# Fifteen small loads of B_x in front of the last three pieces of w4 on the SP queue

## The chip, the cores and the metric

The kernel runs on one core of a Trainium2 chip. The metric is the device time of one execution in microseconds (us). Several executions are timed and the median is given; one further execution is profiled, and all durations inside the kernel come from its trace.

## What is computed

One decoding step: a block of grouped-query attention over a long key and value cache, and a small mixer and MLP beside it, both fed by the same normalized row x of 1024 numbers. Cut to what matters:

```python
def reference(A_x, A_k_cache, A_v_cache, A_wq, A_wo, B_x, B_w1, B_w2, B_w3, B_w4):
    def _A_ref(x, k_cache, v_cache, wq, wo):          # 32 query heads, 4 kv heads, 65536 positions
        q = (x @ wq).reshape(B, Sq, Hq, Dh) ...
        p = softmax(einsum("bhqd,bhkd->bhqk", q, k) * Dh ** -0.5)
        o = einsum("bhqk,bhkd->bhqd", p, v)
        return o.reshape(B, Sq, Hq * Dh) @ wo
    def _B_ref(x, w1, w2, w3, w4):                    # w3: 1024 x 3584, w4: 3584 x 1024
        h = gelu(layernorm(x) @ w1)
        x1 = x + shifted(h) @ w2
        return x1 + gelu(layernorm(x1) @ w3) @ w4
    xn = layernorm(A_x)
    return A_x + _A_ref(xn, A_k_cache, A_v_cache, A_wq, A_wo) + _B_ref(xn, B_w1, B_w2, B_w3, B_w4)
```

All inputs are bf16. The two caches are 64 MiB each, the weights some 30 MiB together. `B_x` is an argument of 1024 numbers that the result doesn't depend on: the B branch is fed by the normalized `A_x`.

## The kernel before

Everything is read from HBM once, in one fixed order, through eight slots of 16 KiB per partition in SBUF (`slots_sb`). All large loads are issued by SP's queue, one after the other. A load of key blocks, of wq, of w3 and the first load of w4 takes two neighbouring slots and moves 4 MiB (3.5 MiB for w3, L302); a load of value blocks, w1, w2 or wo takes one slot and moves 2 MiB (L293). Each has 128 rows, one per partition.

The order is written out by hand in a list `loads`: wq, w1, w2, w3, then group by group the key blocks and the value blocks of the group before, with a wo block when a head is done. It ends with the four value blocks of the last group, the last wo block and w4. A second list, `uses`, gives the order in which the loads are worked on. After every use a helper, `issue()`, puts further loads on SP's queue as long as slots are free in program order; the instruction on the queue then waits on semaphores until the engines have really finished with the slot.

w4 comes in three steps. Its group 0 (rows of the product 0 to 15 in each partition) is one load of two slots. Groups 2 and 3 are cut into pieces by `w4_split` and `load_pieces` (L317), each piece with a semaphore of its own, so that the product can begin with the first piece: group 2 has four pieces of 512 KiB (128 rows of 4096 bytes), group 3 one of 512 KiB and two of 256 KiB (128 rows of 2048 bytes). `load_pieces` first waits for the slot (`_deps`) and then issues its pieces back to back.

On the compute side VectorE transposes the key blocks in 32 x 32 blocks (L522), TensorE forms scores (L529) and the weighted sums of the values (L575), ScalarE takes exponentials (L553). The products with wo and w4 add into one PSUM tile, `M1_ps` (L440). After the last w4 piece, VectorE adds the residual (`fin`, L678), and SP stores the row of 1024 numbers as four rows of 512 bytes (L679) and waits until it has landed.

Two small loads of `A_x` are issued at the start by ScalarE's queue: `xP_bf`, 128 rows of 16 bytes (L391), and `xr_bf`, four rows of 512 bytes (L393).

Of the kernel before, what the change touches and what calls it, by code (L numbers as in the profile page):

```python
# [6 lines left out]
BF = mybir.dt.bfloat16  # L7
# [67 lines left out]
def _deps(q, reads, writes):  # L75
    for b in reads:
        for s, v in b.w.items():
            q.wait((s, v))
    for b in writes:
        for s, v in b.w.items():  # L80
            q.wait((s, v))
        for s, v in b.r.items():
            q.wait((s, v))


def _done(ev, reads, writes, partial=False):
    for b in reads:
        b.add_read(ev)
    for b in writes:
        if partial:  # L90
            b.add_write(ev)
        else:
            b.set_write(ev)
# [24 lines left out]
def _dma(q, chan, fn, reads=(), writes=(), partial=False):  # L118
    _deps(q, reads, writes)
    chan.n += 1  # L120
    ev = q.dma(fn, chan.sem, 16 * chan.n)
    _done(ev, reads, writes, partial)
    return ev
# [10 lines left out]
def bass_parallel_sum__gqa_block_cached__mixer_s_mlp__decode_kernel(  # L134
# [40 lines left out]
    with ExitStack() as es:  # L175
# [3 lines left out]
        def sb(name, shape, dt):  # L179
            return E(nc.sbuf_tensor(name, shape, dt))  # L180
# [4 lines left out]
        def sem(name):  # L185
            return E(nc.semaphore(name))
# [53 lines left out]
        ge_b = sb("ge_b", [P, NT], F32)  # L240
        h1g_bf = sb("h1g_bf", [P, R], BF)
        gh_bf = sb("gh_bf", [P, NT + 32], BF)
        fin = sb("fin", [P, RW], BF)

        S_all = ps("S_ps", [P, NCH * 512], F32)
# [9 lines left out]
        q_pool = _Q("pool", sem("c_pool"))  # L255
        q_sp = _Q("sp", None)
        ch_x = _DmaChan(sem("d_x"))
        ch_out = _DmaChan(sem("d_out"))
        slots = [_Slot(slots_sb[:, i, :], _B("slot%d" % i), _DmaChan(sem("d_s%d" % i))) for i in range(NS)]

# [35 lines left out]
        def load2(src, half=SLOT):  # L296
            i = take(2, 1)
            view = slots_sb[:, i:i + 2, :].rearrange("p s c -> p (s c)")[:, 0:2 * half]
            if 2 * half < 2 * SLOT:
                for k in range(2):  # L300
                    taken[i + k] = 2
            _dma(q_sp, slots[i].chan, lambda e, view=view, src=src: e.dma_start(out=view, in_=src), writes=[slots[i].buf, slots[i + 1].buf])  # L302
            bufs = [[slots[i].buf], [slots[i + 1].buf]] if half == SLOT else [[slots[i].buf, slots[i + 1].buf]] * 2
            return [(view[:, k * half:(k + 1) * half], bufs[k], i + k) for k in range(2)]

        def load_pieces(pieces, width):
            at = take(1, 1)
            sl = slots[at]
            n_load[0] += 1
            _deps(q_sp, [], [sl.buf])  # L310
            bufs = []
            for i, (dst_fn, srcs) in enumerate(pieces):
                ch = _DmaChan(sem("d_p%d_%d" % (n_load[0], i)))
                b = _B()
                for dst, src in dst_fn(sl.view, srcs):
                    ch.n += 1
                    ev = q_sp.dma(lambda e, dst=dst, src=src: e.dma_start(out=dst, in_=src), ch.sem, 16 * ch.n)  # L317
                b.set_write(ev)
                bufs.append([b])
            return sl.view[:, 0:width], bufs, at  # L320
# [16 lines left out]
        w4_split = {2: [2, 2, 2, 2], 3: [2, 1, 1]}  # L337

        def load_w4(grp):
            if grp == 0:  # L340
                return [(v, [(b, 0, R)], i) for v, b, i in load2(w4_v[:, 0:2 * SLOT])]
            n = min(R, NT - grp * R)
            src = w4_v[:, grp * SLOT:grp * SLOT + n * D]
            pieces, at_, k0 = [], [], 0
            for k in w4_split[grp]:
                pieces.append((lambda view, c, src=src: [(view[:, c[0]:c[1]], src[:, c[0]:c[1]])], (k0 * D, (k0 + k) * D)))
                at_.append((k0, k))
                k0 += k
            view, bufs, i = load_pieces(pieces, n * D)
            return [(view, [(bu, k0, k) for bu, (k0, k) in zip(bufs, at_)], i)]  # L350
# [259 lines left out]
        for g in range(NG):  # L610
# [8 lines left out]
            if g > GPH and g % GPH == 1:  # L619
# [8 lines left out]
            reads=[b_xr, b_ln], writes=[b_accr])  # L628
        _op(q_dve, lambda e: e.tensor_tensor(out=accr[:], in0=accr[:], in1=xr_bf[:], op=ALU.add), reads=[b_xr, b_accr], writes=[b_accr])
        loaders = {"wq": load_wq, "w1": lambda: load(w1_v[:, 0:SLOT]), "w2": lambda: load(w2_v[:, 0:SLOT]), "w3": load_w3, "wo": load_wo, "w4": load_w4,  # L630
                   "k": load_k, "v": load_v}
        doubles = {"wq", "w3", "k"}
# [45 lines left out]
        _op(q_dve, lambda e: e.tensor_tensor(out=fin[:], in0=accr[:], in1=M1_ps[:, 0:RW], op=ALU.add), reads=[b_accr, b_M1], writes=[b_fin])  # L678
        ev_out = _dma(q_sp, ch_out, lambda e: e.dma_start(out=out[0, 0, :].rearrange("(j m) -> j m", j=4), in_=fin[0:P:32, :]), reads=[b_fin])  # L679
        q_sp.wait(ev_out)  # L680

        block.sync(lambda e: q_sp.emit(e))
        block.tensor(lambda e: q_pe.emit(e))
# [31 lines left out]
```

## Time and profile before

| what | value |
|---|---|
| median of three timed executions | 406.2 us (406.18 to 406.21) |
| the profiled execution's own time | 406.29 us |
| its span, first to last instruction | 404.6 us |
| HBM read | 169.87 MB, 420 GB/s over the span |
| busy: PE, DVE, ACT, POOL | 170.8, 200.4, 65.2, 7.5 us |
| packets on queue q1 (SP's) | 9512, 98.5% of 16 engines' span |
| packets on q8 and q14 (instruction fetches) | 13 of 16 KB, 5 of 8 KB in the span |
| last waits of TensorE in the last 10 us | 7.6 us for loads of w4 |

PE is TensorE's matmul, DVE VectorE, ACT ScalarE, POOL GpSimd, SP SyncE; a q behind an engine's name means its queue of instructions. The page cuts the span into 40 slices of about 10 us. Beside the page the trace has the start, length and size of each packet of the DMA engines and the time at which each semaphore is raised. A large transfer raises its semaphore sixteen times, once for each DMA engine; it has landed with the sixteenth. Where times such as "first arrival" are given, they are read from there. They count from the span's start.

### The profile page before, as it was taken

How to read it: one execution, taken by the hardware profiler on the slowest of the kernel's cores; microseconds unless marked ns; L12 is line 12 of the kernel's file. 1: busy time of each engine (PE TensorE's matmuls, PEld its weight loads, DVE VectorE, ACT ScalarE, POOL GpSimd, SP SyncE). 2: the span in 40 equal slices, each digit the busy share in tenths (PEclk: the TensorE clock that was granted, in tenths of full speed). 3: DMA queues.
4: the chain of work that ended last, by engine and by line, in shares of the span. 5: the costliest groups of instructions: out<-in, count | busy, mean ns of one | idle time of the engine just before them, and what ended most of it. 6: DMA issues, size and time to landing. Idle time of an engine off the chain costs nothing.

```text
span 404.6 us, 4047 instructions
## 1 busy us (share of the span) xinstructions
PE 170.8 (42%) x1651; PEld 75.4 (19%) x1651; DVE 200.4 (50%) x304; ACT 65.2 (16%) x91; POOL 7.5 (2%) x38
## 2 busy tenths in 40 slices
PE   0273231223555345435335363535252436355626
PEld 0122110102212112211121131212121122122313
DVE  0255027667667665755173737571545655740010
ACT  1000000006007105200610041106010232034000
POOL 5000000000000000000000000000000000000000
PEclk9985655555655965665556655656565657655656
DMA  8999999999999999999999999999999999999995
GB/s 357 421 415 426 452 415 444 413 437 420 462 400 431 429 447 411 441 414 444 411 450 410 437 424 441 415 427 439 423 433 434 423 434 424 420 434 420 444 405 197
DMA packets 9682, 170.13 MB, mean 421 GB/s; under 512 B 1208, under 2 KB 1216, under 8 KB 2112
## 3 DMA queue, kind: packets, MB, share of 16 engines
q1 hardware_dynamic: 9512, 169.88, 98.5%
q8 instruction: 13, 0.21, 0.2%
q14 instruction: 5, 0.04, 0.0%
q10 hardware_dynamic: 152, 0.00, 0.0%
HBM read 169.87 MB, written 0.00 MB: 420 GB/s over the span
## 4 chain that ended last, share of the span: by engine, by line
DMA 57%; DVE 21%; PE 13%; issue 6%; ACT 2%; SPq 0%; POOL 0%; ACTq 0%
DMA slots_sb<-in_A_k_cache_dram 47%; DVE X L522 17%; PE S_ps L529 8%; DMA slots_sb<-in_B_w_dram 7%; DMA xr_bf<-in_A_x_dram 3%; DVE mcol L534 3%; PE OT_ps L575 2%; PE S_ps L440 2%; ACT p_sb L553 1%; ACT pT_sb L565 1%; PE PT_ps L562 1%; PE M_ps L424 0%; PE M_ps L416 0%; PE M_ps L543 0%; SPq L317 0%
## 5 line engine op out<-in xcount | busy, mean ns | idle before, releaser
L522 DVE STREAM_TRANSPOSE X<-slots_sb 128x1024 f32<-128x1024 f32 x128 | 147.7, 1211 | 39.1 <-DMA slots_sb<-in_A_k_cache_dram 39.1
L529 PE MATMUL S_ps<-X,Yall 128*32 128x512 bf16 x512 | 59.9, 614 | 150.4 <-DVE X L522 150.4
L553 ACT ACTIVATE p_sb<-S_ps,brun 128x512 bf16<-128x512 f32 x32 | 45.2, 1412 | 195.5 <-DVE brun L545 105.2
L575 PE MATMUL OT_ps<-slots_sb,pT_sb 128*32 128x512 bf16 x512 | 55.9, 584 | 12.8 <-ACT pT_sb L565 9.6
L534 DVE TENSOR_REDUCE mcol<-S_ps 128x1 f32<-128x512 f32 x32 | 22.1, 692 | 69.2 <-PE S_ps L529 69.2
L529 PEld LDWEIGHTS S_ps<-X,Yall 128*32 128x32 bf16 x512 | 17.3, 126 | 185.8 <-DVE X L522 169.4
L575 PEld LDWEIGHTS OT_ps<-slots_sb,pT_sb 128*32 128x32 bf16 x512 | 18.5, 132 | 37.9 <-issue 32.2
L565 ACT ACTIVATE pT_sb<-PT_ps 128x1024 bf16<-128x1024 bf16 x16 | 16.4, 1023 | 55.6 <-PE PT_ps L562 55.6
L562 PE MATMUL PT_ps<-ident_bf,p_sb 128*128 128x128 bf16 x128 | 15.3, 294 | 11.8 <-ACT pT_sb L565 8.9
L440 PE MATMUL S_ps<-slots_sb,xn_bf 128*32 128x512 bf16 (+1 forms) x128 | 12.6, 567 | 10.7 <-DMA slots_sb<-in_B_w_dram 9.2
L562 PEld LDWEIGHTS PT_ps<-ident_bf,p_sb 128*128 128x128 bf16 x128 | 11.4, 133 | 20.3 <-ACT pT_sb L565 11.0
L592 DVE TENSOR_TENSOR O_acc<-O_acc,OT_ps 128x512 f32<-128x512 f32 x4 | 2.8, 688 | 16.5 <-PE OT_ps L575 16.5
L440 PE MATMUL M_ps<-slots_sb,gh_bf 128*32 128x256 bf16 x112 | 6.5, 399 | 7.7 <-DMA slots_sb<-in_B_w_dram 7.6
L444 DVE STREAM_TRANSPOSE X<-S_ps 128x512 f32<-128x512 f32 (+1 forms) x3 | 2.5, 848 | 14.2 <-PE S_ps L440 14.2
L452 ACT ACTIVATE ge_a<-ge_b 128x8 f32<-128x8 f32 (+1 forms) x2 | 0.4, 217 | 52.2 <-DVE ge_b L451 52.2
L678 DVE TENSOR_TENSOR fin<-accr,M_ps 128x256 bf16<-128x256 f32 x1 | 0.4, 421 | 16.3 <-PE M_ps L440 16.3
L553 ACT ACTIVATION_READ_ACCUMULATOR p_sb<-S_ps,brun 128x1 f32 x32 | 8.5, 264 | 0.0
L440 PE MATMUL M_ps<-slots_sb,oP_bf 128*32 128x256 bf16 x128 | 7.7, 420 | 1.4 <-DVE oP_bf L604 1.4
L597 PE MATMUL M_ps<-O_acc,selX 128*128 128x128 f32 x32 | 8.2, 439 | 0.0
L440 PEld LDWEIGHTS S_ps<-slots_sb,xn_bf 128*32 128x32 bf16 x128 | 4.3, 133 | 17.0 <-DMA slots_sb<-in_B_w_dram 9.9
L597 PEld LDWEIGHTS M_ps<-O_acc,selX 128*128 128x128 f32 x32 | 7.3, 333 | 0.0
L395 DVE CAST xP<-xP_bf 128x8 f32<-128x8 bf16 x1 | 0.2, 172 | 14.2 <-DMA xr_bf<-in_A_x_dram 14.2
(97 smaller groups left out, 70.1 us busy)
## 6 DMA issues: line engine op xcount, KB each, us to landing
slots_sb<-in_A_k_cache_dram SPq DMA_DIRECT2D x16, 4096.0 KB, 26.9
slots_sb<-in_A_v_cache_dram SPq DMA_DIRECT2D x32, 2048.0 KB, 30.7
slots_sb<-in_A_wq_dram SPq DMA_DIRECT2D x2, 4096.0 KB, 16.8
slots_sb<-in_A_wo_dram SPq DMA_DIRECT2D x4, 2048.0 KB, 27.5
slots_sb<-in_B_w_dram SPq DMA_DIRECT2D x2, 3584.0 KB, 33.5
slots_sb<-in_B_w_dram SPq DMA_DIRECT2D x2, 2048.0 KB, 28.1
slots_sb<-in_B_w_dram SPq DMA_DIRECT2D x1, 4096.0 KB, 31.9
slots_sb<-in_B_w_dram SPq DMA_DIRECT2D x5, 512.0 KB, 32.4
```

The lines of the kernel that those rows point to most:

```text
L440: e.matmul(out_fn(j), st_fn(kk), mv_fn(kk, j), start=st, stop=sp, tile_position=(0, 32 * j), skip_group_check=True))
L444: _op(q_dve, lambda e: e.transpose(out=X32[:, 1, c0:c0 + 32 * n], in_=src), reads=b_src, writes=[b_X[1][0]], partial=c0 > 0)
L452: _op(q_act, lambda e: e.activation(a_, bb_, ACTF.Tanh, scale=math.sqrt(2.0 / math.pi)), reads=[b_ge], writes=[b_ge])
L522: _op(q_dve, lambda e, ix=ix: e.transpose(out=X32[:, m, 1024 * ix:1024 * (ix + 1)], in_=K32[:, 1024 * ix:1024 * (ix + 1)]), reads=b, write ...
L529: fns.append(lambda e, we=we, c_mid=c_mid, mv=mv: e.matmul(S_ps[ch][32 * c_mid:32 * c_mid + 32, :], Yall[:, h, we, :, :].rearrange("p a g ...
L534: _op(q_dve, lambda e: e.reduce_max(mcol[:, gm, ch:ch + 1], S_ps[ch][:, :], axis=AX.X), reads=[b_S[ch]], writes=[b_mcol[gm]], partial=ch > 0)
L553: _op(q_act, lambda e, ch=ch: e.activation(p_sb[:, :, :, ch], S_ps[ch][:, :].rearrange("p (c i) -> p c i", i=32), ACTF.Exp, bias=brun[:, k ...
L562: _grp(q_pe, [lambda e, i=i, c=8 * c8 + i: e.transpose(out=PT_ps[:, i * P:(i + 1) * P], in_=p_sb[:, c, :, :].rearrange("p i h -> p (i h)") ...
L565: _op(q_act, lambda e, c8=c8, m=m: e.activation(pT_sb[:, m, :, 32 * c8:32 * c8 + 32, :].rearrange("p a x g -> p x a g"), PT_ps[:, :].rearr ...
L575: fns.append(lambda e, cl=cl, q4=q4: e.matmul(OT_ps[32 * q4:32 * q4 + 32, :], pT_sb[:, m, a, 4 * cl:4 * cl + 4, :].rearrange("p x g -> p ( ...
L592: _op(q_dve, lambda e: e.tensor_tensor(out=O_acc[:, :], in0=O_acc[:, :], in1=OT_ps[:, :], op=ALU.add), reads=[b_OT], writes=[b_O])
L597: fns.append(lambda e, t=t: e.matmul(M0_ps[:, 256:384], selX[:, t, :, :].rearrange("p g x -> p (g x)"), O_acc[:, t * P:(t + 1) * P], start ...
```

## The change

A tile `pr` of 16 partitions x 4096 numbers is added, and a semaphore for it. When `load_w4` is called for group 3, and before `load_pieces` waits for the slot, fifteen loads are issued on SP's queue. Load k (k from 1 to 15) copies the first k x w numbers of `B_x` as k rows of w = 32 + 8 (16 - k) numbers to k partitions of `pr`, at column 256 k. So the rows are 304 bytes long for k = 1 and 16 bytes shorter each time, down to 80 bytes for k = 15; together 120 rows. Nothing reads `pr`. At the very end, behind the wait for the output, SP waits until all fifteen have landed.

```diff
+        pr = sb("pr", [16, 4096], BF)
...
+        ch_pr = _DmaChan(sem("d_pr"))
...
         def load_w4(grp):
+            if grp == 3:
+                for k in range(1, 16):
+                    w = 32 + 8 * (16 - k)
+                    _dma(q_sp, ch_pr, lambda e, k=k, w=w: e.dma_start(out=pr[0:k, 256 * k:256 * k + w], in_=B_x[0, 0, 0:k * w].rearrange("(k w) -> k w", w=w)))
             if grp == 0:
                 return [(v, [(b, 0, R)], i) for v, b, i in load2(w4_v[:, 0:2 * SLOT])]
...
         q_sp.wait(ev_out)
+        q_sp.wait((ch_pr.sem, 16 * ch_pr.n))
```

## The prediction

> **What bounds the kernel now.** The first view is the slices of the span.
>
> ```profile
> DMA  8999999999999999999999999999999999999995
> GB/s 357 421 415 426 452 415 444 413 437 420 462 400 431 429 447 411 441 414 444 411 450 410 437 424 441 415 427 439 423 433 434 423 434 424 420 434 420 444 405 197
> ```
>
> The 16 DMA engines are busy in every slice but the last. TensorE is busy 42% of the span and VectorE 50%, so the time is that of 169.9 MB at about 430 GB/s, plus a head and a tail. Second, the end of the chain of waits in order of time (start, length, what):
>
> ```profile
> 373.34 0.43 SPq L317
> 373.77 0.04 issue
> 373.81 27.82 DMA slots_sb<-in_B_w_dram
> 401.64 0.04 issue
> 401.68 0.32 PE M_ps L440 x4
> 402.00 0.02 issue
> 402.03 0.42 DVE fin L678
> ```
>
> The last piece of w4 is issued at 373.81 and lands 27.82 us later. Behind it stand four matmuls, one addition and the store. What delays that landing delays the end by as much. Third, the SP queue's timeline, its waits from 363 us on, and its issues at L317 in three windows (shortest/median/longest ns):
>
> ```profile
> 362.12 0.33 SPq L302 DMA_DIRECT2D slots_sb<-in_B_w_dram  x1
> 363.81 16.12 SPq L317 DMA_DIRECT2D slots_sb<-in_B_w_dram  x7
> 402.48 0.65 SPq L679 DMA_DIRECT2D out_dram<-fin  x1
> ...
> SPq L48 <- PE OT_ps L575: 7.3, 1, 7.3
> ...
> L317 SPq DMA_DIRECT2D slots_sb<-in_B_w_dram x4: 328/424/432, 363.8 to 365.1; - x4
> ...
> L317 SPq DMA_DIRECT2D slots_sb<-in_B_w_dram x2: 327/381/435, 373.0 to 373.3; - x2
> ...
> L317 SPq DMA_DIRECT2D slots_sb<-in_B_w_dram x1: 6115/6115/6115, 373.8 to 373.8; - x1
> ```
>
> SP issues the four pieces of group 2 until 365.56, waits 7.3 us for a slot, and issues the three pieces of group 3 at 372.97, 373.34 and 373.81. The last issue takes 6.1 us instead of 0.4: the queue holds no more, and it ends 0.6 us after the V block issued at 349.50 has landed on its last engine (379.32). I read that from the trace's semaphore arrivals, sixteen per transfer, one for each engine. They also give the second fact I need: on the last piece the first engine arrives at 398.35 and the sixteenth at 401.64. Five engines come within 0.15 us of the first, six only 2.9 to 3.3 us after it. This spread grows with the 16 KB instruction fetches (thirteen on queue q8): each sets one engine back, the one at 300.07 for instance from 1.50 to 3.04 us. So most engines are done early and the late six make the end.
>
> **The change, step by step.**
>
> *Issue.* No wait precedes the fifteen loads, so they follow the fourth piece of group 2 at 365.56, where SP now idles until 372.92. An issue of 128 rows costs 0.33 to 0.43 us; the two issues of four rows cost 0.65 (the store, L679) and 1.07 (L393 on ACT, while SP was issuing too). I take 0.65 as nearest, on the same queue: 15 x 0.65 = 9.8 us, to 375.3; at 1.07 it is 16.1 us, to 381.6. The first three pieces that stand behind them slip by 2 to 9 us. Nobody waits for these issues: on the first engine the turn of group 3 comes at 395.74, when the transfer before it arrives. Cover 395.74 - 381.6 = 14 us at the dear price; if it were gone, each us would count. On the path: 0.
>
> *Room on the queue.* In the trace a transfer of 128 rows is nine packets on each engine (eight rows and a 4-byte semaphore write). At 373.34 a tenth open transfer, so about 90 packets, was accepted; the eleventh was held. A small load is two packets on each engine that it uses, at most 30 for all fifteen, as much as 3.3 large transfers. The last piece would then be held until three or four more have left: not 379.3 but past the wo load (384.21), the double block of w4 (393.98) and one piece (395.26), so issued by about 396. Data follow an issue by 0.6 us (the store: issue ends at 403.12, first packet at 403.72). Its turn comes at 397.68 on the earliest engine and at 401.0 on the late ones. Cover 397.68 - 396.6 = 1.1 us on early engines, over 4 us on late ones. On the path: 0.
>
> *The engines' own time.* The loads are 120 rows of 80 to 304 bytes. For a row the trace has 7 to 9 ns (16 bytes, L391), 27 ns (512 bytes, L393) and 84 ns (2048 bytes, L317); for a semaphore packet 9 ns, with the next row starting 5 or 6 ns after it. Lower bound: an engine that carries none, 0. Upper bound by rows: the engine with all fifteen, each at the 2048-byte price, 15 x (84 + 9) = 1.4 us. In bytes they are nearest the 512-byte row: 27 + 9 = 36 ns, so 0.54 us for fifteen. Whether the late six are those with many rows the trace doesn't say, since it doesn't number the engines. I take half of fifteen: **+0.25 us**.
>
> The Trainium skill (DMA: Bandwidth & Descriptors, "Why a DMA increments its semaphore by 16 and not by 1") says that a load of k rows runs on the lowest-numbered k engines, the remaining 16 - k increments being written at once by the sequencer. This trace agrees on the count: the store of four rows shows one early semaphore event at 403.50 and four at 404.08 to 404.15. By that rule the fifteen loads heap on the first engines, and the sum would be 0.54 us if such an engine is a late one and 0 if only the highest are.
>
> *Latency at the end.* One more wait stands behind the wait for the output. All small loads landed long before; such a met wait costs about 0.05 us in the chain (0.02 busy and 0.03 issue at L48). **+0.05 us**. The new tile and the new semaphore move no work; 0 to 0.1 us, taken as 0. The 16 added instructions may cause one 8 KB fetch (0.31 to 0.42 us in the trace on one engine), hidden unless it falls on one of the six late engines; taken as 0.
>
> *Sum.* The profiled execution took 406.29 us (span 404.6, 1.7 around it), 0.09 above the median. 406.29 + 0.25 + 0.05 = 406.6 against its own time; against the median of 406.2 that is **406.5**. Its own range is 406.1 to 407.0. A measurement of this kernel can tell about 0.2% (0.8 us) from no change.
>
> **Rivals.**
>
> *A, small packets run dear on a late engine (slower).* If an engine keeps only so many packets in flight, tiny ones use up the places without filling the time. First packets of the kernel took 1.8 to 2.1 us against 1.21 later, so a read has up to 0.85 us of latency to cover. Against: 2048-byte rows follow one another every 80 ns with no gap. If every packet, semaphores too, cost 84 ns: 30 x 84 = 2.5 us on an engine with all rows. It decides from 0.8 us on a late engine, which needs 53 ns per row. Between 0.8 and 2.5, say +1.5: 407.7.
>
> *B, completions in series (slower).* Each load ends with a semaphore write that may hold the next load of the engine until its data are confirmed. The last semaphore packet starts at 401.20 and its arrival is at 401.64, so 0.43 us; fifteen in a row are 6.5 us on one engine: 3.2 us beyond the end if it is an early engine, 6.5 if a late one, so 409.4 to 412.7, say 411. For: nowhere in the trace do two semaphore writes of one engine stand closer than 0.6 us. Against: the row behind a semaphore packet starts 6 ns later, and does not wait for it. It decides from 0.05 us per load on a late engine. The Trainium skill (DMA: Bandwidth & Descriptors, "Anatomy of one DMA — SWDGE (gpsimd) path") puts about 2 us of fixed cost on every DMA, mostly confirmation of the last write; were that paid in a row, fifteen would be an estimated 30 us, and here the three last pieces, arriving 0.5 to 0.64 us apart, speak against it.
>
> *C, the queue counts transfers (slower).* If it holds nine or ten whatever their size, the fifteen take the places of large ones. With nine open, the ninth small load is issued when the last piece of group 2 arrives (399.07); the six behind it and the three pieces need 6 x 0.43 to 6 x 0.65 and 3 x 0.4 us. With 0.6 us to the first packet, 1 MB at 430 GB/s (2.4) and 0.4 to the arrival, the end moves from 401.64 to between 406 and 407.4: +4.4 to +5.8, say 411.4. It decides from the moment when the last issue falls behind 400. For: the held eleventh issue. Against: a large transfer left at 374.28 and the issue was still held until 379.9, which a plain count doesn't explain.
>
> *D, an issue is dearer than any shown (slower).* Odd row counts with a new row length each time might cost more at the issue. From 2 us per load the last pieces come after 397 and the backlog runs dry; at 2.5 us, 365.56 + 37.5 + 1.2 + 2.9 = 407.2 instead of 401.64: 411.8. No issue in the trace but the held one is over 1.1 us.
>
> *E, faster.* No work goes. Only instruction fetches falling on other engines could bring the late six forward, and they follow TensorE's program, which stays. 405.3 or less.
>
> **How the numbers follow.** Forecast 0.59, A 0.14, B 0.10, C 0.09, D 0.04, E 0.04. So within 0.2%: 0.59; slower: 0.14 + 0.10 + 0.09 + 0.04 = 0.37; faster: 0.04. The forecast is the likeliest, 406.5. The range begins at 406.1, the median less what one measurement spreads, and must reach B and C, since A alone leaves 0.23 beyond it: 411.5 covers A, C's middle and most of B.
>
> **What would show it.** Right: fifteen issues between 365.6 and 382 at 0.4 to 1.1 us each; the last piece issued before 397.7; its first arrival near 398.4 and its last at 401.6 to 402.2; the small packets two by two without gaps. A shows as gaps between them, B as gaps of 0.4 us behind each semaphore packet, C as small issues that end one by one with landings and DMA idle behind 399, D as long issues with the queue not full. The forecast is wrong if the last piece lands past 402.4.

## The result and the profile after

The changed kernel takes 407.63 us (median of five, 407.54 to 407.87) against 406.2 (median of five, 406.18 to 406.21): a ratio of 1.0035, 95% interval 1.0024 to 1.0045. It is slower by 1.43 us, more than the 0.8 us that a measurement can tell from no change. The profiled execution took 407.54 us, its span is 405.8 us, 1.2 us longer than before.

The slices of the span after:

```profile
DMA  9999999999999999999999999999999999999994
GB/s 362 414 417 432 439 417 459 405 430 430 443 415 449 405 436 423 452 409 436 416 439 423 441 413 443 416 431 431 436 422 434 418 454 409 424 431 422 441 404 152
```

The stream is the same up to the last slice, where 152 GB/s stand in place of 197. The end of the chain of waits after (start, length, what), and SP's timeline:

```profile
385.45 0.02 SPq L48
385.47 0.03 issue
385.50 2.31 SPq L319
387.81 0.04 issue
387.86 1.40 SPq L319
389.25 0.04 issue
389.30 13.44 DMA slots_sb<-in_B_w_dram
402.73 0.04 issue
402.78 0.43 PE M_ps L446 x4
403.21 0.02 issue
403.24 0.42 DVE fin L684
```

```profile
363.76 1.75 SPq L319 DMA_DIRECT2D slots_sb<-in_B_w_dram  x4
365.55 19.85 SPq L345 DMA_DIRECT2D pr<-in_B_x_dram  x15
385.50 6.61 SPq L319 DMA_DIRECT2D slots_sb<-in_B_w_dram  x3
403.68 0.62 SPq L685 DMA_DIRECT2D out_dram<-fin  x1
```

The fifteen issues held SP for 19.85 us, and the three pieces were issued at 385.5 to 389.3 instead of 373. The last piece landed at 402.73 instead of 401.64: 1.09 us of the 1.2. The trace has the sixteen arrivals of that piece: fifteen engines had landed by 401.67, the sixteenth alone came at 402.73. The remaining 0.11 us is the last group of four matmuls, 0.43 us instead of 0.32. In the stretches of 2.5 us that hold it, TensorE's clock was granted at 1.00 before and at 0.50 after. Each line below has a stretch, its length, the busy time of PE, PEld (weight loads), DVE, ACT and POOL with the number of instructions, the granted clock, the DMA share and GB/s; the first fence is the kernel before:

```profile
395.00:397.50 2.50, 2.50 (x56) 1.84 (x52) 0.00 (x0) 0.00 (x0) 0.00 (x0) 0.50 1.04 410
397.50:400.00 2.50, 2.02 (x36) 0.84 (x28) 0.00 (x0) 0.00 (x0) 0.00 (x0) 0.51 0.65 245
400.00:402.50 2.50, 0.99 (x16) 0.33 (x16) 0.42 (x1) 0.00 (x0) 0.00 (x0) 1.00 0.15 56
```

```profile
395.00:397.50 2.50, 2.50 (x56) 1.87 (x48) 0.00 (x0) 0.00 (x0) 0.00 (x0) 0.50 1.06 340
397.50:400.00 2.50, 1.44 (x36) 0.70 (x28) 0.00 (x0) 0.00 (x0) 0.00 (x0) 0.89 0.87 272
400.00:402.50 2.50, 0.98 (x12) 0.25 (x12) 0.00 (x0) 0.00 (x0) 0.00 (x0) 0.80 0.28 102
402.50:405.00 2.50, 0.45 (x8) 0.11 (x4) 0.42 (x1) 0.00 (x0) 0.00 (x0) 0.50 0.00 1
```

From 395.0 to 397.5 the changed kernel shows its engines busy (share 1.06) while only 340 GB/s move; the kernel before moved 410 there, at a share of 1.04. So the packets of this stretch last longer than their bytes need. The trace has each packet's length, and the fifteen row lengths tell each load's packets apart: load k leaves packets on k engines, one each, and an engine that has a row of load k has one of every later load. So one engine carries fifteen, the next fourteen, and so on down to none. On the engine with fifteen the small rows start 18 ns after one another (395.521 to 395.776), with the semaphore writes between them. Behind them stand rows of w4 that last far longer than the 0.16 us of a 4096-byte row. Six of the sixteen engines are shown; on the one with fifteen only the first row could be followed:

```
one engine each: small loads carried, the w4 rows behind them (r: 0.16 us, | semaphore write, h: 0.08 us)
15   908 ns in the first row
11   r  796  r r r r r  755 |  255 h h h h h h h | h h h h h h h h |
 8   r  296  r r r r r  866 |  271 h h h h h h h | h h h h h h h h |
 7   r  198  r r r r r  462 |  231 h h h h h h h | h h h h h h h h |
 5   r r r r r r r  194 |  232 h h h h h h h | h h h h h h h h |
 3   r r r r r r r r | h h h h h h h h | h h h h h h h h |
```

Of the 640 rows of 4096 bytes, none was over 175 ns before and 25 are now, by 11.7 us together (beyond 0.16 us each). The engine that ended last has 649 ns in the last row ahead of a semaphore write and 238 ns in the row behind it. By elimination it is the engine with twelve: of the five late engines its small packets began first, at 398.13, and the four others (six, five, four and three small loads) began at 398.3 to 398.6 and ended before 401.3, it at 402.32. The prediction counted six late engines in the kernel before; the sixth is the one on which the instruction fetch of 398.3 falls (1.10 us). That fetch stands at 398.3 in both kernels, so it isn't the difference.

### The profile page after: what moved, and what is told of

The parts are those of the page before. It is cut to its first block, busy times and chain, and to the rows that moved or that the text cites. A ratio compares the mean times of both kernels' runs of the same rounds, so it can differ in the third digit from the quotient of the medians.

```text
span 405.8 us, 4063 instructions
## 1 busy us (share of the span) xinstructions
PE 167.1 (41%) x1651; PEld 74.5 (18%) x1651; DVE 200.3 (49%) x304; ACT 64.9 (16%) x91; POOL 7.5 (2%) x38
## 4 chain that ended last, share of the span: by engine, by line
DMA 54%; DVE 21%; PE 12%; SPq 6%; issue 6%; ACT 1%; POOL 0%; ACTq 0%
DMA slots_sb<-in_A_k_cache_dram 47%; DVE X L528 17%; PE S_ps L535 7%; SPq L345 5%; DMA xr_bf<-in_A_x_dram 3%; DMA slots_sb<-in_B_w_dram 3%; DVE mcol L540 3%; PE OT_ps L581 2%; PE S_ps L446 1%; SPq L319 1%; PE M_ps L446 1%; ACT pT_sb L571 1%; PE PT_ps L568 1%; PE M_ps L430 0%; PE M_ps L422 0%
## 5 line engine op out<-in xcount | busy, mean ns | idle before, releaser
L581 PE MATMUL OT_ps<-slots_sb,pT_sb 128*32 128x512 bf16 x512 | 54.6, 570 | 13.9 <-ACT pT_sb L571 9.6
```

The costliest lines, as they stand in the source:

```text
L581: fns.append(lambda e, cl=cl, q4=q4: e.matmul(OT_ps[32 * q4:32 * q4 + 32, :], pT_sb[:, m, a, 4 * cl:4 * cl + 4, :].rearrange("p x g -> p ( ...
```

## Experiments

Theory 1: small packets in a run make the w4 rows behind them wait. Theory 2: the last pieces are issued too late, since SP is held. Theory 4: differing lengths and row counts are dear. The numbers are those of the expectations; there is no theory 3. Each kernel ran against the kernel before on the same chip, whose median was 406.32 to 406.35 there. The table gathers what was measured; "slow" are rows of 4096 bytes over 175 ns, "excess" what they take beyond 0.16 us, summed over all engines.

```
run         median   ratio to before (95%)     slow  excess us  longest ns  last w4 row ends
e_late      406.29   1.0000 (0.9991, 1.0010)      0     0.0        -          401.06
e_behind    406.38   1.0001 (0.9991, 1.0010)      0     0.0        -          401.05
e_same      408.35   1.0049 (1.0034, 1.0064)     25    17.0      1244         402.95
e_five      406.48   1.0003 (0.9994, 1.0013)     16     1.1       356         401.23
e_even      408.64   1.0058 (1.0043, 1.0073)     50    33.3      1144         403.42
e_one15     406.75   1.0010 (1.0001, 1.0020)     44     2.3       347         401.57
e_early     407.55   1.0030 (1.0018, 1.0042)      0     0.0        -          402.53
e_act       406.54   1.0004 (0.9994, 1.0013)      4     0.1       193         401.25
e_even_w    408.74   1.0061 (1.0046, 1.0076)     49    30.6      1006         403.41
e_sems      407.50   1.0030 (1.0018, 1.0042)     24    10.9       949         402.29
e_spread    406.48   1.0003 (0.9994, 1.0013)     14     0.4       240         401.25
e_22        410.24   1.0095 (1.0079, 1.0112)     55    57.3      2512         405.25
```

**Late issue alone.** The kernel before, with one more wait:

```diff
         def load_w4(grp):
+            if grp == 3:
+                q_sp.wait(hold[0])      # the event that writes oP_bf of the last head
...
```

In the lines left out here `hold` is filled, and group 3 isn't put on the queue before it is.

> No small loads; the three pieces of group 3 are issued only when the last head's oP_bf is done (about 385.5, where the changed kernel issues them), instead of 373. Theory 1 (small packets in the queue use up the engines' read-ahead, and the w4 rows behind them wait for their data): no row of w4 over 175 ns, time as before, 406.2 +- 0.2. Theory 2 (the last pieces are issued too late because the small issues hold SP for 20 us): about ten to twenty rows of 0.4 to 0.9 us as in the changed kernel, time 407.3 to 407.8.

The pieces were issued at 385.19, 385.56 and 386.04, and the last landed 15.47 us later:

```profile
385.56 0.43 SPq L317
385.99 0.04 issue
386.04 15.47 DMA slots_sb<-in_B_w_dram
401.51 0.04 issue
```

401.51 is as early as in the kernel before. No row is slow. Theory 2 falls: 12 us of lateness on SP cost nothing. (The changed kernel issued its last piece later still, at 389.3; the run with the loads spread out goes beyond that.)

**Behind instead of in front.** The loop stands behind `load_pieces`, else as in the change.

> The same fifteen loads, issued behind the three pieces of group 3 instead of in front of them. Theory 1: no row of w4 stands behind a small packet, so no slow row; time 406.2 to 406.5 (the wait at the end, and the small packets of the late engines if they land after the output). Theory 2: the pieces are issued at 373 again, 406.2 to 406.5 as well. If it is 407 or more, both fall: then the loads cost by being in the queue at all.

Same time, no slow row. The loads as such cost nothing; they must stand in front of something. The wait at the end costs nothing that can be measured either.

**Equal loads.**

```diff
-                    w = 32 + 8 * (16 - k)
-                    ... out=pr[0:k, 256 * k:256 * k + w], in_=B_x[0, 0, 0:k * w] ...
+                    ... out=pr[0:8, 256 * k:256 * k + 96], in_=B_x[0, 0, 0:8 * 96] ...
```

> Fifteen loads of 8 rows of 192 bytes each, all alike (120 rows as in the change, but on eight engines only and of one length). Theory 1: what counts is the number of small packets on the late engines; the late engine 3 has 15 instead of 12: 407.5 to 408.0. Theory 4 (the differing lengths and row counts make issues or packets dear): issues back near 0.35 to 0.65 us and time 406.2 to 406.7.

2.0 us slower than before, a little more than forecast. Theory 4 falls: equal lengths take nothing off. ("Late engine 3" in the expectation is the one that carries twelve small loads in the changed kernel; here it carries fifteen.) That the number on the late engines counts fits this run, in which the time grew with that number.

**Five loads.** `range(11, 16)` in place of `range(1, 16)`.

> Only the five loads of 11 to 15 rows: 65 rows, at most five small packets with data per engine. Theory 1: in the changed kernel engines with up to five small loads had nearly no slow row, so 406.3 to 406.6. Theory 2: SP is held for about 7 instead of 20 us and the pieces are issued at about 373, so 406.2 to 406.5. A cost per load (1.43 / 15 = 0.095 us each) would give 406.7.

The time can't be told from the kernel before. Its interval (up to 1.0013, 0.5 us) doesn't exclude 0.095 us per load, but the trace speaks against it: the last piece landed at 401.62, as before (401.64), and the slow rows have 1.1 us together instead of 11.7. Five loads on an engine are nearly free.

**Sixteen rows each.**

```diff
+                    ... out=pr[0:16, 256 * k:256 * k + 64], in_=B_x[0, 0, 0:1024].rearrange("(k w) -> k w", w=64)
```

> Fifteen loads of 16 rows of 128 bytes, so each of the 16 engines carries fifteen small loads (240 rows). If the stall belongs to small packets (data and semaphore write together): every late engine stalls as the engines with fifteen did in the run with equal loads, 0.27 us of packets and about 1.0 to 1.9 us of waiting rows, 407.8 to 408.8. If a load cost by its issue or its odd row count, this would be no dearer than the change: 407.6 or less.

With fifteen on every engine the cost is 2.3 us, with about three slow rows per engine.

**One load with the same number of small data packets.**

```diff
-        pr = sb("pr", [16, 4096], BF)
+        pr = sb("pr", [16, 15, 80], BF)
...
+                _dma(q_sp, ch_pr, lambda e: e.dma_start(out=pr[:, :, 0:64], in_=B_w1[0:16, 0:960].rearrange("p (k w) -> p k w", w=64)))
```

> One load in place of fifteen: 16 rows of fifteen separate runs of 128 bytes, so each engine gets fifteen small data packets as in the run before, but a single semaphore write. If the stall comes from small data packets using up the read-ahead: 407.3 to 408.5, rows of 4096 bytes over 0.5 us on most engines. If it comes from the row of semaphore writes (fifteen completions close together): 406.2 to 406.6 and no slow row.

This run turned theory 1 around. Fifteen small data packets per engine, 9 ns apart, cost 0.4 us, not 2.3. The time lies between the two forecasts, and there are slow rows where the second had none, but the longest took 0.35 us. Fourteen ends of transfers less, with their semaphore writes, took nearly all of the cost away. The small excess spread over 44 rows (2.3 us over 16 engines) stays for the packets themselves.

A rival would be that small packets of both kinds count, data and semaphore writes alike: an engine has 16 here and 30 in the run before. The trace of the changed kernel speaks against it. Its engine with eight loads has 16 small packets too, and its rows of 296 and 866 ns are 0.84 us over; here an engine has 0.15 us on average.

**The same packets from the same addresses, fifteen loads.** The run above differs from the even one in its source too, so:

```diff
-        pr = sb("pr", [16, 4096], BF)
+        pr = sb("pr", [16, 15, 80], BF)
...
+                for k in range(15):
+                    ... out=pr[:, k, 0:64], in_=B_w1[0:16, 64 * k:64 * k + 64]
```

> The same 240 pieces of 128 bytes of w1 as in the run with one load of 16 x 15 runs, but as fifteen loads of 16 rows: the same data packets from the same addresses on every engine, fifteen semaphore writes instead of one. If the semaphore writes (the ends of transfers) cost: 408.4 to 408.9, as the even run that read B_x. If the cost came from all engines reading the same 2 KB of B_x: 406.5 to 407.0, as the run with one load.

2.4 us, as the even run. The addresses don't matter; the ends of transfers do, each with one semaphore write on each engine. The runs don't separate the write from whatever else belongs to the end of a transfer.

```profile
391.61 12.20 DMA slots_sb<-in_B_w_dram
403.81 0.04 issue
403.85 0.43 PE M_ps L445 x4
```

The last piece lands at 403.81 here, 2.2 us behind the kernel before.

**A semaphore for each load.** Fifteen channels in place of one.

> The change as it is, but each of the fifteen loads has a semaphore of its own. If the ends of transfers cost as such: 407.4 to 407.9, as the change. If many engines raising one and the same semaphore at once were the cost: 406.3 to 406.7.

As the change. It is not that many engines raise one semaphore.

The run shows something more. With a semaphore for each load, the trace tells when each load lands on each engine. On the late engine with twelve small loads (4 to 15), their rows start between 398.195 and 398.385, 17 ns apart. The last arrival of each load, which by the times is that of this engine, comes far more slowly:

```
load          4        5        6        7        8        9       10       11       12       13       14       15
arrival 398.865  399.050  399.232  399.410  399.602  399.793  399.984  400.177  400.370  400.552  400.732  400.912
```

These are 0.18 to 0.19 us from one to the next, 2.05 us for eleven steps. So the ends of the transfers are worked off one after the other, while the packets behind them have already started. The sixteenth arrival of the next piece of w4 is at 401.383, 0.47 us after the last of these.

**Seven more.** Twenty-two loads of 16 rows of 128 bytes of w1 (each source row overlaps the next load's by half).

> Twenty-two loads of 16 rows instead of fifteen (as the run with fifteen that reads w1, seven more). Each end of a transfer worked off in series at about 0.15 us, and 0.02 us of packets: 7 x 0.17 = 1.2 us more than with fifteen, 409.5 to 410.1. A stop that is paid once after a run, however long: 408.6 to 408.9.

410.24, above the range. Against fifteen it is 1.50 us for seven loads, 0.21 us each; the rows' excess per engine grows from 1.9 to 3.6 us, 0.24 each. So the stop is not paid once: the ends are worked off one after the other. The 0.21 us are close to the 0.19 us between two arrivals in the run before and the 0.018 us that a small load's packets take. If the cost grows in a straight line, at 0.21 us each the 2.39 us of fifteen are eleven, and about four are free; that is an estimate. The pieces were issued only at 393.9 to 394.8 here. They were issued before the first slow row (395.4), but this run alone can't exclude a part of lateness.

**In front of the large rows.** The loop runs for group 0 instead of group 3.

> The fifteen loads of the change stand in front of group 0 of w4, whose rows are 32 KB, and behind the wo block with rows of 16 KB. If the read-ahead holds a number of packets, a few large rows already cover the wait, so hardly any stall: 406.2 to 406.7. If it is a fixed stop after a run of small packets whatever follows: 407.2 to 408, as in the change, since the engines never catch up behind it.

The first theory falls: rows of 32 KB don't cover the wait. 19 of them took 1.33 to 2.68 us instead of 1.21, 12.4 us more together, and the kernel takes 1.2 us longer, as with the change. The delay of these rows, at 380.4 to 386.0, is still there at the end: the last piece landed at 403.00 instead of 401.64.

**Spread out.** Three loads behind each of the four pieces of group 2 and the first of group 3.

```diff
+                for _ in range(3):
+                    if todo:
+                        k = todo.pop(0)
+                        _dma(q_sp, ch_pr, ...)
```

> The same fifteen loads, three behind each of the four pieces of group 2 and three behind the first piece of group 3, instead of fifteen in a run. If an engine can work off a few close ends of transfers behind large rows and only a run of more than about four is dear: 406.2 to 406.8. If every end of a transfer costs its 0.1 to 0.15 us wherever it stands: 407.3 to 407.9, as the change.

The time can't be told from the kernel before: the same fifteen loads, the same 120 rows and as many semaphore writes, but no more than three in a row, and between two such groups the 1.3 us of a piece of w4. SP was held here too:

```profile
380.70 9.88 SPq L326 DMA_DIRECT2D pr<-in_B_x_dram  x3
390.63 1.60 SPq L321 DMA_DIRECT2D slots_sb<-in_B_w_dram  x2
```

The last two pieces were issued at 390.6 and 391.1, later than in the changed kernel, and again this cost nothing.

**Another queue.** The same loads from ScalarE, behind its last transposes.

> The same fifteen loads, issued by ScalarE's queue behind its last transposes (from about 371 us). They go through a queue of their own, whose packets alternate with the large rows of SP's queue instead of standing in a run in front of w4. Small packets in a run being the cause: 406.2 to 406.6, no slow row of w4. If it were the small packets as such: 407 or more.

```profile
370.16 5.32 ACTq L671 DMA_DIRECT2D pr<-in_B_x_dram  x15
```

The time can't be told from the kernel before. The 240 packets of the small loads are spread over 373.8 to 392.3 here, among rows of 4, 16 and 32 KB, so the semaphore writes don't stand in a run. They also run earlier than in the change, but the run in front of the large rows shows that an early place alone doesn't make a run of them free.

No version beat the kernel before. Of those that keep all fifteen loads, the spread one, the one behind and the one on ScalarE's queue give the loads away for nothing that could be measured.

## Why the prediction was right and wrong

The range (406.1 to 411.5) held the time, but only because it was stretched beyond the sum's own, 406.1 to 407.0, to cover the rivals. The sum failed: its own range missed, and the forecast, within 0.2%, did not come: the kernel is 0.35% slower. The prediction's own sign of being wrong came too: the last piece landed at 402.73, past 402.4. Point by point:

- *What bounds the kernel* was read rightly. The stream of loads sets the end, and the landing of the last piece on the late engines carried 1.09 of the 1.2 us.
- *Issue*: no effect, as said. The price was mis-sized. Free of a full queue an issue of k rows took 0.24 to 0.38 us (e_early), not 0.65; with the queue full the fifteen took 19.85 us instead of 9.8 to 16.1.
- *Room on the queue*: held. The last piece was issued at 389.3, the issue ended at 392.1, within the "by about 396", and e_late and e_spread show that such lateness is free. Rival C, a queue that counts transfers, is out: it had the ninth small load issued at 399.07, and all fifteen were issued by 385.4. (By its own terms its end comes to 406.2 to 407.6, not 406 to 407.4.)
- *The engines' own time*: this step failed, in its terms "an engine that carries none, 0" to "15 x (84 + 9) = 1.4 us" and the +0.25 us taken from them. The packets were overpriced, 18 ns per small load instead of 36. What the sum put at nothing was larger: the ends of the loads are worked off one after the other, and the w4 rows behind them wait. 25 of these rows took 11.7 us too long together, and the engine that ended last, with twelve small loads, landed 1.09 us later than the last landing before. The prediction had such waits in rivals A and B alone.
- *Rival A* gave the time best, 407.7, but by luck: not for its reason. That the data packets use up places is what e_one15 took away, and its sign, gaps between the small packets, didn't come.
- *Rival B*, completions in series, named the mechanism that the runs support and mis-sized it: 0.19 us from one arrival to the next (e_sems), 0.21 us of time for each load more (e_22) and about four free, in place of 0.43 us for each. Its sign, gaps of 0.4 us behind each semaphore packet, didn't come either: the next small row doesn't wait, and the gaps are between the arrivals. The trace of before spoke against it in my reading, since the row behind a semaphore packet starts 6 ns later. That holds for the small rows here too; what stops is a row of w4 behind them.
- *Rival D*, dear issues, is out by e_early and e_same.
- *Latency at the end*: the extra wait was put at 0.05 us; from the store's issue to the end of the span it is 2.1 us in both kernels.

The Trainium skill (DMA: Bandwidth & Descriptors, "Anatomy of one DMA — SWDGE (gpsimd) path") puts about 2 us of fixed cost on a DMA, most of it the confirmation of the last write. That section is on loads issued by GpSimd; these were issued by SP. These runs show an effect of the ends of transfers too, at a tenth of that: 0.21 us for each when more than about four stand in a run on an engine, and none that could be measured with no more than three in a row and 1.3 us of large rows between (e_spread).

That ends of transfers in a run cost time, and that they arrive one after the other, is shown. How an end that waits holds up the rows behind it isn't: why about four are free, and why the stop falls on the first or second row and on the row ahead of the next semaphore write, was not tried. It stays open.

## What to carry to other kernels

Where the stream of loads is the bound, a run of small transfers on its queue costs through its ends, not through its bytes or its issue time: merge them into one transfer, spread them between large ones, or put them behind the stream or on another queue. Count how many stand in a row on the engine that ends last, not how many there are. A late issue is harmless as long as the backlog on the queue lasts longer: 12 to 17 us later cost nothing here.

## What the runs showed of the hardware that was not expected

- A run of transfers of one small row per engine is drained at 18 ns each, but their ends arrive 0.18 to 0.19 us apart on an engine (e_sems), and the engine stops in later rows: with 22 in a run sixteen rows, as many as there are engines, took 2.06 to 2.51 us, with fifteen (e_even_w) all slow rows but one took 0.5 to 1.0 us, about three on each engine.
- The stop does not shrink with large rows behind it: rows of 32 KB took up to 2.68 us instead of 1.21.
- A load of k rows runs on k engines and the sets are nested: the engines of load k are among those of load k + 1. The Trainium skill (DMA: Bandwidth & Descriptors, "Why a DMA increments its semaphore by 16 and not by 1") says the lowest-numbered k; the trace shows the nesting, not the numbers.
- SP holds an issue when the queue is full by up to 6.2 us for a single small load (e_spread), without any effect on the end.
